# Gate and value products of an attention and GLU kernel's last batch by a seven-product scheme on 2x2 blocks

## The chip, the cores and the metric

The kernel runs on one core of one Trainium2 chip. The metric is the device time of a run in microseconds (us), median over runs; a profile of one execution gives the span from its first to its last instruction, and what each engine did in it. The engines are TensorE (PE in the rows, its weight loads PEld), VectorE (DVE), ScalarE (ACT), GpSimd (POOL) and SyncE (SP), which issues the DMAs here.

## The reference, cut to what matters

Attention on pairwise averaged queries, then a gated product of its result with three weight matrices, all in float32.

```python
B, H, S, D = 4, 8, 1152, 64                    # q, k, v
q_pool = q.reshape(B, H, S // 2, 2, D).mean(axis=3)
attn = softmax(q_pool @ k.T / sqrt(D))         # 576 x 1152 for each head
x = (attn @ v).transpose(0, 2, 1, 3).reshape(2304, 512)
gate = 1.0 / (1.0 + np.exp(-(x @ w_gate)))     # w_gate, w_val: 512 x 1536
out = (gate * (x @ w_val)) @ w_out             # w_out: 1536 x 512
```

## The kernel before

A float32 operand is held as two float32r parts, high and low, and a product is three matmuls into one PSUM bank: high x high, high x low, low x high. Attention goes by pairs of heads (16 pairs `p`, four to a batch) and by halves of 288 queries (`GR`, `GN = 288`). `normalise` writes each pair's result to a tile `x` with its two parts: 128 features, 576 tokens. Four such tiles are the 512 features of one batch.

`gated(ch, ...)` does the products of batch `ch`. Three times (`for th in range(3)`) it takes four of the twelve rows of 128 hidden features: for each row gate and value (`s`), two halves of tokens (`hf`) and four blocks of features (`kc`), three matmuls each; then the output product of these four rows, for four blocks `dm` of the result and two halves. A value product is multiplied with the gate on VectorE (line 895), copied to its high part on ScalarE (line 899), and POOL takes the low part (line 903) into a tile `g`, of which there are four. The output products are summed on VectorE (line 931) and stored after the last third. Weights come in by SyncE from a DRAM copy `w_d` that holds both parts: gate and value weights into three tiles `wg`, output weights into two tiles `wo`, in the last batch into the three pairs `K` (KA, KB) that attention has left by then:

```python
            tag = "K" if kind == "wo" and ch == B - 1 else kind
            wh = pl.hold(tag)
```

Nothing is ordered by hand. Each piece of work is declared with an engine, a guessed duration, a due time and what it must follow (`pl.op`), and each buffer as a slot of a tag (`SLOTS`, `pl.hold`). `Plan.run` lists all of it in time by these guesses, `Plan.search` shuffles due times and keeps what ends earlier, and the resulting order is the program order of every engine; an engine keeps to it. So products of one batch stand among the attention of the next, and what the last batch needs stands alone at the end. There are eight PSUM banks `b`.

Line 646 is the part of attention in which VectorE forms the low part of the exponentials (`el`), lines 465 and 481 form low parts of queries and keys, line 675 on POOL adds up rows of exponentials, and line 804 is a ScalarE copy of 512 weight columns.

## Time and profile before

| | |
|---|---|
| median of 3 runs | 920.87 us (919.88 to 922.19) |
| the profiled execution, first to last instruction | 919.1 us, 1.77 under the median; no other time of this execution is given |
| instructions | 18605 |
| busy: TensorE, VectorE, ScalarE, POOL | 910.0, 649.5, 657.5, 671.1 us |
| TensorE's granted clock | 1.00 of full speed throughout |

Busy times of matmuls overlap each other, since they are pipelined: what a matmul takes is read from how many start in a stretch. In a row of a group stand the line, the engine, the operation, what is written and read, the shape, the count, then the busy time in us and the mean duration in ns, then the idle time of the engine before these instructions and what ended it.

### The profile page before, as it was taken

The page shows a single profiled execution, that of the slowest core. Times are in us where ns is not written, and L with a number is a line of the kernel's source. Part 1 is how long each engine was busy: PE and PEld are TensorE (multiplying, and loading weights), DVE is VectorE, ACT ScalarE, POOL GpSimd, SP SyncE. Part 2 cuts the span into 40 slices and gives each one's busy share as a digit, 9 for nine tenths or more (in the row PEclk, how much of TensorE's full clock was granted, in tenths as well). Part 3 has the DMA queues.
Part 4 walks back from the last instruction along what each step waited for, and adds up shares of the span by engine and source line. Part 5 has one row for each costly group of instructions (what it writes and reads, how often), then busy time and mean ns, then how long its engine had stood idle before and what let it go on. Part 6 is the DMA issues. An engine that isn't in the chain of part 4 may idle for free.

```text
span 919.1 us, 18605 instructions
## 1 busy us (share of the span) xinstructions
PE 910.0 (99%) x6371; PEld 882.8 (96%) x6371; DVE 649.5 (71%) x1427; ACT 657.5 (72%) x1703; POOL 671.1 (73%) x669
## 2 busy tenths in 40 slices
PE   8999999999999999999999999999999999999998
PEld 8888888999999999999999999999999999999998
DVE  6677779888898987878787878877777874510112
ACT  4798899989998886777887677677877767422111
POOL 6765366889888989889899888888889877521211
PEclk9999999999999999999999999999999999999999
DMA  6899888788868666555644455554545423435432
GB/s 140 212 289 247 275 254 261 239 266 273 262 210 275 206 202 192 161 157 149 166 136 142 131 157 157 160 148 132 166 123 158 142 93 115 166 139 183 162 115 75
DMA packets 57616, 166.27 MB, mean 181 GB/s; under 512 B 17393, under 2 KB 21745, under 8 KB 51377
## 3 DMA queue, kind: packets, MB, share of 16 engines
q1 hardware_dynamic: 57360, 164.78, 59.3%
q8 instruction: 50, 0.82, 0.4%
q10 hardware_dynamic: 160, 0.30, 0.1%
q14 instruction: 46, 0.37, 0.1%
HBM read 132.12 MB, written 23.59 MB: 169 GB/s over the span
## 4 chain that ended last, share of the span: by engine, by line
PE 91%; ACT 4%; DVE 3%; POOL 1%; DMA 1%; issue 1%; POOLq 0%; ACTq 0%; DVEq 0%
PE bank L846 47%; PE bank L610 15%; PE bank L504 7%; PE bank L628 7%; PE bank L657 6%; PE bank L653 6%; PE bank L730 1%; DVE pm L417 1%; PE bank L951 1%; DMA wg<-wg_d 1%; ACT eh L614 1%; ACT bank L643 0%; ACT KA L475 0%; DMA wo<-wo_d 0%; DVE el L646 0%
## 5 line engine op out<-in xcount | busy, mean ns | idle before, releaser
L846 PE MATMUL bank<-x,wg 128*128 128x288 f32 x2304 | 353.8, 295 | 0.0
L846 PEld LDWEIGHTS bank<-x,wg 128*128 128x128 f32 x2304 | 325.6, 188 | 1.1 <-ACT sg L889 0.4
L646 DVE TENSOR_TENSOR el<-bank,eh 128x288 fp32r<-128x288 f32 x432 | 192.9, 452 | 70.7 <-ACT bank L643 65.9
L510 DVE TENSOR_REDUCE pm<-bank 128x1 f32<-128x384 f32 (+1 forms) x375 | 199.7, 550 | 49.6 <-PE bank L504 45.0
L614 ACT ACTIVATE eh<-bank 128x288 fp32r<-128x288 f32 x432 | 176.4, 409 | 73.1 <-PE bank L610 65.9
L643 ACT ACTIVATE bank<-bank 128x288 f32<-128x288 f32 x432 | 176.9, 410 | 0.2
L610 PE MATMUL bank<-QA,KA 128*128 128x288 f32 x576 | 175.1, 308 | 1.5 <-DVE pm L510 0.9
L610 PE MATMUL bank<-QB,KB 128*128 128x288 f32 x576 | 167.4, 295 | 0.0
L903 POOL TENSOR_TENSOR g<-sg,g 128x288 fp32r<-128x288 f32 x96 | 79.9, 833 | 105.2 <-ACT g L899 102.7
L675 POOL TENSOR_TENSOR acc<-acc,eh 128x576 f32<-128x576 f32 x92 | 132.5, 1440 | 16.7 <-ACT eh L614 14.6
L846 PE MATMUL bank<-g,wo 128*128 128x288 f32 x864 | 139.2, 295 | 0.2
L657 PE MATMUL bank<-el,vt 128*128 128x288 f32 x432 | 127.2, 296 | 0.5 <-DVE el L646 0.5
L653 PE MATMUL bank<-eh,vt 128*128 128x288 f32 x432 | 127.3, 296 | 0.0
L846 PEld LDWEIGHTS bank<-g,wo 128*128 128x128 f32 x864 | 125.0, 188 | 1.2 <-DMA wo<-wo_d 0.3
L504 PE MATMUL bank<-KA,QA 128*128 128x384 f32 (+1 forms) x375 | 125.7, 350 | 0.2
L610 PEld LDWEIGHTS bank<-QA,KA 128*128 128x128 f32 x576 | 108.2, 188 | 5.9 <-DVE pm L510 1.3
L610 PEld LDWEIGHTS bank<-QB,KB 128*128 128x128 f32 x576 | 108.3, 188 | 1.3
L895 DVE SCALAR_TENSOR_TENSOR sg<-sg,bank 128x288 f32<-128x288 f32 x96 | 43.3, 451 | 81.2 <-PE bank L846 79.2
L657 PEld LDWEIGHTS bank<-el,vt 128*128 128x128 f32 x432 | 81.1, 188 | 1.5 <-DVE el L646 1.2
L653 PEld LDWEIGHTS bank<-eh,vt 128*128 128x128 f32 x432 | 81.1, 188 | 0.7 <-ACT eh L614 0.3
L675 POOL TENSOR_TENSOR acc<-eh,eh 128x576 f32<-128x576 f32 x48 | 68.7, 1431 | 15.6 <-ACT eh L614 10.9
L628 PE MATMUL bank<-e,ve 128*128 128x288 f32 x288 | 76.6, 407 | 0.0
(86 smaller groups left out, 1359.6 us busy)
## 6 DMA issues: line engine op xcount, KB each, us to landing
wg<-wg_d SPq DMA_DIRECT2D x48, 1024.0 KB, 5.2
wo<-wo_d SPq DMA_DIRECT2D x36, 512.0 KB, 3.9
kr<-in_kT_dram SPq DMA_DIRECT2D x62, 288.0 KB, 5.0
wg_d<-cs SPq DMA_DIRECT2D x24, 512.0 KB, 5.0
qr<-in_qT_dram SPq DMA_DIRECT2D x31, 288.0 KB, 4.1
KP<-KA SPq DMA_DIRECT2D x30, 288.0 KB, 4.4
vr<-in_v_dram SPq DMA_DIRECT2D x24, 288.0 KB, 3.1
cr<-in_wg_dram SPq DMA_DIRECT2D x12, 512.0 KB, 5.3
```

What stands on the lines that cost most here:

```text
L504: nc.tensor.matmul(out=tl(m)[LO if t == 4 else ALL, 0:384], lhsT=lhs(t), rhs=rhs()[:, j * 384:(j + 1) * 384], start=True, stop=True)
L510: nc.vector.tensor_reduce(out=o, in_=tl(m)[p, 0:384], axis=AXX, op=ALU.max)
L610: nc.tensor.matmul(out=tl(m)[:, 0:GN], lhsT=tl(hd["k"])[k][:, ks], rhs=tl(hd["q"])[k][:, a:b], start=(k == 0), stop=(k == 1))
L614: nc.scalar.activation(out=ev(), in_=tl(m)[:, 0:GN], func=ACTF.Exp, scale=1.0 / 16.0)
L628: nc.tensor.matmul(out=tl(av[0])[:, 0:GN], lhsT=pair(c, 0), rhs=tl(h), start=(c == 0), stop=(c == NC - 1))
L643: nc.scalar.activation(out=p, in_=p, func=ACTF.Exp, scale=1.0 / 16.0)
L646: nc.vector.tensor_tensor(out=tl(el), in0=tl(m)[:, 0:GN], in1=ev().bitcast(F32), op=ALU.subtract)
L653: nc.tensor.matmul(out=tl(av[0])[:, 0:GN], lhsT=pair(c, w), rhs=ev(), start=(c == 0), stop=(c == NC - 1))
L657: nc.tensor.matmul(out=tl(av[1])[:, 0:GN], lhsT=pair(c, 1 - w), rhs=tl(el), start=(c == 0), stop=(c == NC - 1 and not mine_c))
L675: nc.gpsimd.tensor_tensor(out=tl(acc), in0=tl(old).bitcast(F32), in1=tl(eh).bitcast(F32), op=ALU.add)
L846: nc.tensor.matmul(out=ps[:, 0:GN], lhsT=l, rhs=r, start=(n == 0 and j == 0), stop=(n == 3 and j == 2))
L903: nc.gpsimd.tensor_tensor(out=g[:, 1, a:b], in0=tl(sg), in1=g[:, 0, a:b].bitcast(F32), op=ALU.subtract)
```

## The change

Batches 0 to 2 are as before. In the last batch two rows of hidden features and the 512 features of `x` make a 2x2 block matrix of weights (A11 to A22, blocks of 128 hidden by 256 features), and the features and the two token halves make a 2x2 matrix of `x` (B11 to B22). Seven block products take the place of eight: A11·B11, A12·B21, A22·T4, S1·T1, S2·T2, S3·T3, S4·B22, each of two K halves of 128 features and three matmuls.

The token blocks T1 to T4 are formed once, in `differences`, for the last two pairs: VectorE subtracts in float32, ScalarE makes the high and VectorE the low part. They lie in tiles that attention has left (Q, KP; the float32 work in vr). The weight blocks S1 to S4 are formed twelve times, in `combinations`: VectorE adds high and low part of two rows (line 950) and forms four sums of 256 columns in tile `kr` (line 953); ScalarE copies the high parts and POOL subtracts for the low parts (line 970), into one of the three pairs K. The plain weight rows come into `wg` as before, every fourth into `vt0` and `vt1`. The results are put together on VectorE: from one bank and a running sum in `sg` (line 1014), or within the bank (line 1050), before tanh (gate) or line 1073 (value, as line 895 before). Output weights of the last batch now use the two tiles `wo`.

```diff
+    def differences(p, j, me, nm, s):
+        if j == 0:
+            tb.update({"1": pl.hold("Q"), "2": pl.hold("Q"), "3": pl.hold("KP"), "4": pl.hold("Q"), "f": pl.hold("vr")})
+        old, fh = xs[p - 2, 0], tb["f"]
+        t1 = lambda: tl(fh).rearrange("p c d -> p (c d)")[:, GN * j:GN * j + GN]
+        b1 = lambda l, g: tl(old)[:, l, GN * g:GN * g + GN].bitcast(F32)
+        b21, b22 = (lambda: tl(me)[:, 0:GN]), (lambda: tl(me)[:, GN:SQ])
...
+        o = mix(t1, lambda: b1(0, 1), lambda: b1(0, 0), ALU.subtract, [old] + ([fh] if j else []),
+                [x_done[p - 2, 0], x_done[p - 2, 1]], s - 2, [] if j else [fh])
+        o = mix(t1, t1, lambda: b1(1, 1), ALU.add, [old, fh], [o], s - 2)
+        o = mix(t1, t1, lambda: b1(1, 0), ALU.subtract, [old, fh], [o], s - 2)
+        s1 = split("1", t1, [fh], [o], s)
+        t2 = mix(t1, b22, t1, ALU.subtract, [me, fh], [nm, s1], s)
+        split("2", t1, [fh], [t2], s + 0.1)
+        o = mix(b22, b22, lambda: b1(0, 1), ALU.subtract, [me, old], [t2, x_done[p, 1]], s + 0.1)
+        t3 = mix(b22, b22, lambda: b1(1, 1), ALU.subtract, [me, old], [o], s + 0.1)
+        t4 = mix(b21, b21, t1, ALU.subtract, [me, fh], [t2, x_done[p, 0]], s + 0.2)
+        split("3", b22, [me], [t3], s + 0.2)
+        split("4", b21, [me], [t4], s + 0.3)
...
-            tag = "K" if kind == "wo" and ch == B - 1 else kind
-            wh = pl.hold(tag)
+            wh = pl.hold(kind)
...
+            whs = [pl.hold("vt0"), pl.hold("vt1")] if m_ % 4 == 3 else [pl.hold("wg")]
...
+            fh, sh = pl.hold("kr"), pl.hold("K")
...
+            def full(w, h):
+                nc.vector.tensor_tensor(out=f(h, A), in0=w(0, s, A).bitcast(F32), in1=w(1, s, A).bitcast(F32), op=ALU.add)
+
+            def mix(out, in0, in1, op, after):
+                return pl.op("DVE", dve(256), lambda: nc.vector.tensor_tensor(out=f(*out), in0=f(*in0), in1=f(*in1), op=op),
...
+            r0 = pl.op("DVE", dve(512), lambda: full(a0, f0), at - 7, after=[l0], uses=w0, take=[fh])
+            r1 = pl.op("DVE", dve(512), lambda: full(a1, f1), at - 7, after=[l1], uses=w1 + [fh])
+            s1 = mix((f1, R), (f1, L), (f1, R), ALU.add, [r1])
+            s3 = mix((f1, L), (f0, L), (f1, L), ALU.subtract, [r0, s1])
+            s2 = mix((f0, L), (f1, R), (f0, L), ALU.subtract, [s1, s3])
+            s4 = mix((f0, R), (f0, R), (f0, L), ALU.subtract, [s2])
...
+                o = pl.op("ACT", act(512), hi, at - 6, after=after, uses=[fh] + ([sh] if k else []), take=[] if k else [sh])
+                done.append(pl.op("POOL", pool(512), lo, at - 6, after=[o], uses=[fh, sh]))
...
+            return {"A11": (w0, plain_w(a0, 0), l0), "A12": (w0, plain_w(a0, 256), l0), "A22": (w1, plain_w(a1, 256), l1),
+                    "S3": ([sh], mixed(0, 0), done[0]), "S1": ([sh], mixed(0, 256), done[0]),
+                    "S2": ([sh], mixed(1, 0), done[1]), "S4": ([sh], mixed(1, 256), done[1])}
...
+                    def mm(j=j, x=x):
+                        for c, (h, l) in enumerate(((0, 0), (0, 1), (1, 0))):
+                            nc.tensor.matmul(out=tl(bank)[:, 0:GN], lhsT=w(h, j), rhs=x(l),
+                                             start=(j == 0 and c == 0), stop=(j == 1 and c == 2))
+
+                    last = pl.op("PE", 3 * pe(GN), mm, at + 0.05 * j, after=[last, lw, xd],
+                                 uses=wh + [xh] + ([bank] if j else []), take=[] if j else [bank])
+                return bank, last, at
...
+            b, p, at = mult("A11", "11")
+            k1 = keep(s1, b, [p], at)
+            b, p, at = mult("S2", "T2")
+            k2 = plus(s2, b, s1, [p, k1], at)
+            b, p, at = mult("A12", "21")
+            put(0, 0, b, s1, [p, k1], at)
+            b, p, at = mult("S1", "T1")
+            k4 = plus(s4, b, s2, [p, k2], at)
+            b, p, at = mult("S3", "T3")
+            u2 = plus(s2, b, s2, [p, k2, k4], at)
+            put(1, 1, b, s4, [p, k4, u2], at)
+            b, p, at = mult("S4", "22")
+            put(0, 1, b, s4, [p, k4], at)
+            b, p, at = mult("A22", "T4")
+            put(1, 0, b, s2, [p, u2], at)
...
+                o = add(bank, sh, after, at)
+                done[r, hf] = pl.op("ACT", act(GN), tanh, at - 1, after=[o], uses=[bank] + ([] if new else [f]), take=[f] if new else [])
...
+        for third in range(3):
             gs = {}
-            for m_ in range(4 * th, 4 * th + 4):
+            if ch == B - 1:
+                two_rows(2 * third, gs)
+                two_rows(2 * third + 1, gs)
+            for m_ in range(4 * third, 4 * third + 4 if ch < B - 1 else 0):
```

The matmul's program line was 846 and is 892 for what stays and 1004 for the seven products. On TensorE, the first third was, before, one product after the other with the plain weights (`wg1`, then `wg2`) and the four `x` tiles:

```order
L846 MATMUL bank_69<-x7_128,wg1_133 128x288 x3
L846 MATMUL bank_69<-x0_3945,wg1_133 128x288 x3
L846 MATMUL bank_69<-x1_3946,wg1_133 128x288 x3
L846 MATMUL bank_69<-x6_127,wg2_134 128x288 x3
L846 MATMUL bank_69<-x7_128,wg2_134 128x288 x3
```

Now, the value products of the first two rows, from S1·T1 on (S1 and S3 in KA0, S2 and S4 in KB0, T1 to T4 in QA2 and QB2, QA0 and QB0, KP, QA1 and QB1):

```order
L1004 MATMUL bank_69<-QA2_82,KA0_74 128x288 x3
L1004 MATMUL bank_69<-QB2_85,KA0_74 128x288 x3
L1004 MATMUL bank_69<-KP_116,KA0_74 128x288 x3
L1004 MATMUL bank_69<-QA0_80,KB0_77 128x288 x3
L1004 MATMUL bank_69<-QB0_83,KB0_77 128x288 x3
L1004 MATMUL bank_69<-KP_116,KA0_74 128x288 x3
L1004 MATMUL bank_69<-x0_3921,KB0_77 128x288 x3
L1004 MATMUL bank_69<-x1_3922,KB0_77 128x288 x3
L1004 MATMUL bank_69<-QA1_81,wg1_133 128x288 x3
L1004 MATMUL bank_69<-QB1_84,wg1_133 128x288 x3
```

Eight of these ten rows read a weight sum or a token block that VectorE has made, and the rows are not in the order of the seven products but in the order in which the planner expects their operands.

On VectorE, the same stage was, before, from the end of the attention on (`opart` the last output products of batch 2, `sg` the value products of the last batch):

```order
L931 SCALAR_TENSOR_TENSOR opart2_131<-bank_69,opart2_131 128x288
L931 SCALAR_TENSOR_TENSOR opart3_132<-bank_69,opart3_132 128x288 x2
L895 SCALAR_TENSOR_TENSOR sg0_142<-sg0_142,bank_69 128x288
L895 SCALAR_TENSOR_TENSOR sg1_143<-sg1_143,bank_69 128x288
L895 SCALAR_TENSOR_TENSOR sg2_144<-sg2_144,bank_69 128x288
```

Now, from the sums for the second pair's gate on, with what each waits for:

```order
L950 TENSOR_TENSOR kr0_86<-wg2_134 128x512 [waits DMAHW7_49,Pool_49]
L950 TENSOR_TENSOR kr0_86<-vt00_89 128x512 [waits DMAHW4_49]
L1014 TENSOR_TENSOR sg2_144<-bank_69,sg0_142 128x288 [waits PE_49]
L953 TENSOR_TENSOR kr0_86<-kr0_86 128x256 [waits DVE_49] x4
L1014 TENSOR_TENSOR sg1_143<-bank_69,sg2_144 128x288
L1014 TENSOR_TENSOR sg2_144<-bank_69,sg2_144 128x288 [waits DVE_49,PE_49]
L1050 TENSOR_TENSOR bank_69<-bank_69,sg1_143 128x288
L1073 SCALAR_TENSOR_TENSOR t0_102<-t0_102,bank_69 128x288 [waits DVE_49,Activation_49]
L1050 TENSOR_TENSOR bank_69<-bank_69,sg1_143 128x288 [waits PE_49]
L1073 SCALAR_TENSOR_TENSOR acc0_99<-acc0_99,bank_69 128x288 [waits DVE_49,Activation_49]
L1050 TENSOR_TENSOR bank_69<-bank_69,sg2_144 128x288 [waits PE_49]
```

The first row waits for POOL to leave `kr`, and the additions that free banks stand behind it.

On SyncE, the last output weights were, before, loaded into three tiles in turn:

```order
L862 DMA KA0_74<-wo_d_146 128x1024
L862 DMA KA1_75<-wo_d_146 128x1024
L862 DMA KA2_76<-wo_d_146 128x1024
L862 DMA KA0_74<-wo_d_146 128x1024
L862 DMA wg2_134<-wg_d_145 128x2048
L942 DMA out_0_dram<-opart0_129 128x288
L862 DMA KA1_75<-wo_d_146 128x1024
```

Now they are loaded into two (these rows begin with the last third's first load):

```order
L906 DMA wo0_135<-wo_d_146 128x1024
L906 DMA wo1_136<-wo_d_146 128x1024
L906 DMA wo0_135<-wo_d_146 128x1024
L1170 DMA out_0_dram<-opart0_129 128x288 x2
L906 DMA wo1_136<-wo_d_146 128x1024
L1170 DMA out_0_dram<-opart1_130 128x288 x2
```

The third and the fourth load each go into a tile that the first and the second block of the same third have just read.

## Rows read from the trace of the kernel before

**Rows 1.** The page's part 1: busy us, share of the span, instructions.

```profile
span 919.1 us, 18605 instructions
...
PE 910.0 (99%) x6371; PEld 882.8 (96%) x6371; DVE 649.5 (71%) x1427; ACT 657.5 (72%) x1703; POOL 671.1 (73%) x669
```

**Rows 2.** Windows of the run: busy us and rows of each engine, granted clock.

```profile
core 0: us, PE busy (x) PEld busy (x) DVE busy (x) ACT busy (x) POOL busy (x), PEclk, DMA share, GB/s
...
500.00:600.00 100.00, 99.81 (x735) 99.30 (x734) 81.62 (x184) 73.08 (x196) 86.50 (x85) 1.00 0.55 162
...
740.00:760.00 20.00, 20.00 (x149) 20.00 (x148) 15.90 (x38) 14.79 (x40) 15.70 (x19) 1.00 0.24 93
760.00:780.00 20.00, 20.00 (x153) 20.00 (x153) 9.08 (x22) 14.38 (x42) 14.52 (x15) 1.00 0.36 132
...
820.00:840.00 20.00, 20.00 (x153) 20.00 (x152) 1.36 (x3) 5.04 (x12) 3.22 (x4) 1.00 0.52 185
```

**Rows 3.** The chain that ended last, from 850 us on.

```profile
849.89 66.01 PE bank L846 x498
...
915.93 0.46 DVE opart L931
```

**Rows 4.** Groups by line and shape, 787 us to the end.

```profile
L846 PE MATMUL bank<-x,wg 128*128 128x288 f32 x576 | 77.0, 295 | 0.0
...
L903 POOL TENSOR_TENSOR g<-sg,g 128x288 fp32r<-128x288 f32 x24 | 19.4, 807 | 84.6 <-ACT g L899 84.6
...
L931 DVE SCALAR_TENSOR_TENSOR opart<-bank,opart 128x288 f32<-128x288 f32 x24 | 11.0, 457 | 24.1 <-PE bank L846 24.0
L895 DVE SCALAR_TENSOR_TENSOR sg<-sg,bank 128x288 f32<-128x288 f32 x24 | 10.9, 454 | 76.7 <-PE bank L846 76.7
```

**Rows 5.** Groups by line and shape, the whole run.

```profile
L646 DVE TENSOR_TENSOR el<-bank,eh 128x288 fp32r<-128x288 f32 x432 | 192.9, 452 | 70.7 <-ACT bank L643 65.9 <-PE bank L504 0.3
...
L675 POOL TENSOR_TENSOR acc<-eh,eh 128x576 f32<-128x576 f32 x48 | 68.7, 1431 | 15.6 <-ACT eh L614 10.9 <-PE bank L504 2.1 <-PE bank L846 1.0
...
L804 ACT ACTIVATE cs<-bank 128x512 fp32r<-128x512 f32 x36 | 21.5, 609 | 0.3 <-DVE bank L800 0.2
...
L481 DVE TENSOR_TENSOR KB<-kr,KA 64x576 fp32r<-64x576 f32 x16 | 16.3, 1019 | 0.5
...
L465 DVE TENSOR_TENSOR QA<-qr,QA 64x576 fp32r<-64x576 f32 x16 | 15.3, 955 | 1.0 <-ACT opart L929 0.5
...
L370 DVE TENSOR_TENSOR qr<-qr 64x384 f32<-64x384 f32 x1 | 0.6, 550 | 1.9 <-DMA qr<-in_qT_dram 1.9
...
L370 DVE TENSOR_TENSOR qr<-qr 64x192 f32<-64x192 f32 x1 | 0.4, 351 | 0.4 <-DMA qr<-in_qT_dram 0.4
```

**Rows 6.** Line 481 on VectorE: duration in ns, min, median, max.

```profile
L481 DVE TENSOR_TENSOR KB<-kr,KA x16: 755/963/1925, 323.5 to 727.3; 64x576 fp32r<-64x576 f32 x16
```

**Rows 7.** VectorE in order of time: start us, duration us, and the instruction.

```profile
252.01 0.45 DVE L646 TENSOR_TENSOR el<-bank,eh 128x288 fp32r<-128x288 f32 x1
252.38 0.45 DVE L895 SCALAR_TENSOR_TENSOR sg<-sg,bank 128x288 f32<-128x288 f32 x1
...
253.90 0.46 DVE L646 TENSOR_TENSOR el<-bank,eh 128x288 fp32r<-128x288 f32 x1
254.39 0.46 DVE L709 TENSOR_TENSOR y<-bank,t 64x288 f32<-64x288 f32 x1
```

**Rows 8.** All engines in order of time, after one value product.

```profile
846.03 0.46 DVE L895 SCALAR_TENSOR_TENSOR sg<-sg,bank 128x288 f32<-128x288 f32 x1 [1.14 <-PE bank L846]
846.52 0.44 ACT L899 ACTIVATE g<-sg 128x288 fp32r<-128x288 f32 x1 [1.15 <-DVE sg L895]
847.11 0.81 POOL L903 TENSOR_TENSOR g<-sg,g 128x288 fp32r<-128x288 f32 x1 [0.78 <-ACT g L899]
```

**Rows 9.** DMA issues: count, KB each, median us from issue to landing.

```profile
wo<-wo_d SPq DMA_DIRECT2D x36, 512.0 KB, 3.9
...
KA<-wo_d SPq DMA_DIRECT2D x12, 512.0 KB, 3.3
```

More of the change, by code (lines that the diff above doesn't have):

```diff
@@ L757, in mult @@
             nc.gpsimd.tensor_tensor(out=y, in0=y, in1=tl(st["r"])[:, a:b], op=ALU.mult)
-        nm = pl.op("DVE", 1.2 if NMP(p) else 1.65, norm, s, after=st["yo"][g], uses=[st["y"], st["r"]], take=[th])
+        nm = pl.op("DVE", 1.2 if NMP(p) else 1.65, norm, s, after=st["yo"][g], uses=[st["y"], st["r"]], take=[tth])
         if NMP(p):
@@ L831, in gated, with now @@
         acc = {}
[L833 to L835 removed]
+        def now(n=1.0):
+            n_g[0] += n
+            return base + step * (n_g[0] - n)
         def product(at, parts, uses, after):
@@ new lines, in seven, with mult, plus, add @@
+        def seven(i, s, put):
+            sw = combinations(i, s)
+            s1, s2, s4 = (pl.hold("sg") for _ in range(3))
+            def mult(wname, name):
+                at = now(0.5)
+                wh, w, lw = sw[wname]
+                bank, last = pl.hold("b"), None
+                for j in range(2):
+                    if name in ("11", "21", "22"):
+                        p, hf = 4 * ch + 2 * (name[0] == "2") + j, int(name[1] == "2")
+                        xh, xd = xs[p, 0], x_done[p, hf]
+                        x = lambda l, xh=xh, hf=hf: tl(xh)[:, l, hf * GN:hf * GN + GN]
+                    else:
+                        xh, xd = tb[name[1]], x_done[name, j]
+                        x = lambda l, xh=xh, j=j: t_block(xh, j)[:, l]
+                    def mm(j=j, x=x):
[5 more added lines that the diff above has]
+                return bank, last, at
+            def plus(out, bank, sh, after, at):
+                def add():
+                    nc.vector.tensor_tensor(out=tl(out), in0=tl(bank)[:, 0:GN], in1=tl(sh), op=ALU.add)
+                return pl.op("DVE", dve(GN), add, at - 1, after=after, uses=[bank, sh],
+                             take=[] if out is sh else [out])
+            def keep(out, bank, after, at):
+                def copy():
+                    nc.scalar.activation(out=tl(out), in_=tl(bank)[:, 0:GN], func=ACTF.Copy)
+                return pl.op("ACT", act(GN), copy, at - 1, after=after, uses=[bank], take=[out])
+            b, p, at = mult("A11", "11")
[13 more added lines that the diff above has]
+            put(1, 0, b, s2, [p, u2], at)
@@ L911, in gated @@
             for dm in range(4):
-                wh, wt, lw = weights("wo", 4 * th + dm, base + step * n_g[0])
-                if th == 0:
+                wh, wt, lw = weights("wo", 4 * third + dm, base + step * n_g[0])
+                if third == 0:
                     acc[dm] = [pl.hold("opart"), [None, None]]
@@ L938, in gated @@
                     prev[hf] = o
-                    if th == 2:
+                    if third == 2:
                         def store(dm=dm, oh=oh, a=a, b=b):
@@ L978, in attention_glu_kernel @@
             pl.op("SP", 0.0, change_pools, PB + 1, after=[o for l in stored.values() for o in l], uses=blocked)
+        for some in later:
+            differences(*some)
         gated(b, PB * (b + 1), PB)
```

113 lines of the change are left out of this document (101 added, 12 removed).

## The prediction

> **What bounds the kernel now.** First the page's busy line: TensorE is busy 910.0 of 919.1 us, the next engines about 73% [rows 1]. A sum over stages hides where there is room, so the windows come second: from 740 us on TensorE is busy 20.00 of 20 at granted clock 1.00 (the 2.4 GHz level), while VectorE falls from 15.90 (740 to 760) to 1.36 (820 to 840), when the last batch's products are all that is left [rows 2]. Third, the chain that ended last: 66.01 us of nothing but 498 matmuls of line 846, then one VectorE instruction of 0.46 us and its store [rows 3]. So in the last stage a matmul less is time less, and a product of 128x288 costs 66.01 / 498 = 0.1326 us (the 295 ns in the groups overlap each other). The other engines wait there: lines 895 and 931 for TensorE nearly all the time [rows 4].
>
> **The part removed.** Before, the last batch's gate and value products are the 576 matmuls of [rows 4]. After, six pairs of weight rows x gate or value x seven products x two halves of K x three float32r terms = 504. 72 x 0.1326 = **9.55 us**, and TensorE has no idle time there that could swallow it.
>
> **What VectorE gets.** One third of the stage is four weight rows and their share of the output product: 168 + 96 = 264 matmuls, 35.0 us. VectorE does in it, before: eight of line 895 and eight of line 931, 8 x 0.454 + 8 x 0.457 = 7.3 us [rows 4]. After, for each of four combinations (line 950 twice on 512 columns, line 953 four times on 256): no row has these shapes, but line 370 takes 351 and 550 ns for 192 and 384 columns [rows 5], 1.04 ns a column, and the shortest 576 of line 481, 755 ns [rows 6], lies on that line; so 0.68 and 0.42, together 3.04 us. For each of the 28 products one addition out of a bank at line 646's 0.452 [rows 5]. Sum: 4 x 3.04 + 28 x 0.452 + 7.3 = **32.1 us against TensorE's 35.0**. Independent instructions start 0.37 apart, dependent ones 0.49 [rows 7], so full durations are a fair middle. VectorE goes from 7.3 of 38.2 us (288 matmuls), 19%, to 92% of the stage and stays 2.9 us a third under TensorE: hidden on the average, with little left. POOL: eight of 512 columns, between 0.807 at 288 and 1.431 at 576 [rows 4, 5], so 1.29, and eight of 0.807: 16.8 of 35.0. ScalarE gets four copies of at most 0.61 [rows 5] a pair of weight rows and is not near a bound.
>
> **How a sum comes in time.** One combination is 2 x 0.68 + 2 x 0.42 on VectorE, a ScalarE copy of at most 0.61, two POOL subtractions of 1.29 that follow each other, and handovers of 0.03 and 0.15 between engines [rows 8]: about 5.6 us from first addition to last low part, and tile kr is held throughout. TensorE eats one in 42 matmuls, 5.6 us. They tie, and three K pairs let the sums run ahead only while output products (12.7 us a third) run. Following the change's order with these durations from the attention's end, I find S products late by about 0.4 us in the first third, when the second pair's sums follow the first's additions, and not after. The first addition of the next sum waits for POOL to free kr, and behind it on VectorE stand additions that free banks; that is the place where 0.4 could grow (the second rival).
>
> **Collisions.** All sums of weights have both inputs in SBUF, as lines 481 and 465 on VectorE. These average 1.019 and 0.955 against a shortest of 0.755, with one of 1.925 [rows 5, 6]: 0.20 to 0.26 us extra, in stretches where POOL is busy 86.5% [rows 2]. The stage's POOL share is 16.8 / 35.0 = 48%, so some 0.13 each: 24 x 0.13 = 3.1 us a third, just the slack. I charge TensorE 0.5 a third, **1.5 us**; bounds 0, and 24 x 0.26 less 2.9 = 3.3 a third, 10.
> The Trainium skill, SBUF — State Buffer, "Who interferes with whom", says that a VectorE instruction with two SBUF inputs and a GpSimd instruction that reads SBUF exclude each other for the whole instruction; the spread of line 481 agrees in kind. By that rule, if every one of the 72 waited for half a POOL subtraction at a 48% chance, it would be 0.31 us each, 22 us: a slower kernel, about 925 us.
>
> **Token sums.** 14 differences and 8 low parts for each of the last two pairs' blocks, 22 x 0.45 = 9.9 us, and the first weight sum of 3.0, lie before the attention's end, where VectorE has 4.1 + 10.9 us free in 740 to 780 [rows 2]. Cost 0; uncovered, each would hold an `el` and so TensorE by 0.45. Behind the last normalisation the first T2 product waits for a difference, a copy and a low part (0.45 + 0.44 + 0.45) where x waited for copy and POOL (0.44 + 0.81) [rows 4, 8], one handover more, with 36 matmuls of cover in the order: 0.2, bounds 0 and 1.
>
> **The end of the last third.** After the last S2·T2 come 27 matmuls; VectorE has eleven instructions for them, 5.0 us, then the copy and the low part, 1.4 with handovers: 6.4 us before the last g is there. TensorE has 27 + 18 matmuls, 6.0: **0.5 us** of wait, in a place that had none. And the output weights: before, three KA tiles; now two wo tiles, and dm 2 can be loaded only when dm 0's last matmul is over. 24 matmuls, 3.2 us, must hide a transfer of 3.3 (KA) to 3.9 us (wo) [rows 9]: **0.4**, bounds 0.1 and 0.9. In the first two thirds other products stand between.
>
> **The rest of the program** is put in a new order by the same planner, since all queues are planned at once. TensorE is idle there about 0.2% (99.81 of 100 in 500 to 600 [rows 2]); I take 0, and 1 us to both sides.
>
> **Sum.** -9.55 + 0.4 + 1.5 + 0.2 + 0.5 + 0.4 = -6.55: span 919.1 to 912.55. The median of the runs, 920.87, is 1.77 above this span; the profiled execution has no other time of its own. **914.3 us.**
>
> **Rivals.**
> *All of it arrives.* No wait but the 0.5 at the end: -9.0, 911.8. For it: VectorE's sum is still under TensorE's. Against: two chains tie with TensorE.
> *Each sum is late.* The tie breaks the wrong way: each of twelve combinations is late by 0.5 us (one VectorE addition ahead of it in the queue), 6 us instead of 1.9: 918.4, no difference to speak of. For it: kr is single and VectorE keeps its order. Against: output products give every third 12.7 us to catch up.
> *VectorE becomes the bound.* It decides where the 72 weight sums wait for POOL by more than (3 x 2.9 + 9.55) / 72 = 0.25 us each; at 0.35, between line 481's mean and its longest, the stage is 25.2 - 18.2 = 7 us longer than before: 928, slower. For it: rows 6 and 92% before any wait. Against: POOL is half as busy as where these rows come from.
> The rule in the section on collisions is this rival.
>
> **Numbers.** Chances: forecast 0.65 (its bounds: 910.8 with every wait at its lower end and 1 us of luck in the new order, 917.5 with collisions at 4.5), all 0.15, late sums 0.13, VectorE 0.07. A measurement of this kernel tells about 0.3% from no change, 2.8 us: faster is under 918.1. The first two and a quarter of the third are faster, 0.82; the third's remainder and little else the same, 0.10; slower 0.08. Range 910.8 to 919.5, leaving out the top of the late sums and the slow case.
>
> **What would show it.** In the changed profile: 504 matmuls of the new line; TensorE nearly unbroken from 790 us on with VectorE at 85 to 95%; lines 950 and 953 at 0.68 and 0.42 with a tail; waits of TensorE for POOL on KA and KB under 2 us in all; a wait for wo near the end. Wrong would be TensorE waiting for VectorE's additions (banks) all through the stage, or lines 950 and 953 at half again their price, or losses of more than 1 us before 740.

## The result, and the profile after

The change made the kernel slower: 930.51 us, median of four runs (929.62 to 931.79), against 921.25 us for the kernel before on the same chip, a ratio of 1.0101 (95% interval 1.0087 to 1.0115): 1% slower. The forecast was 914.3. The profiled execution spans 929.6 us, 10.5 more than the one before. The 72 matmuls are gone (6371 before, now 6299), and with them 9.55 us; so 20.0 us were lost somewhere in this execution (18.8 by the medians).

The busy line of the page after, the answer to [rows 1]:

```profile
PE 909.1 (98%) x6299; PEld 873.3 (94%) x6299; DVE 742.1 (80%) x1605; ACT 679.3 (73%) x1747; POOL 706.7 (76%) x693
```

TensorE has 72 matmuls less and is busy just as long: the busy time of matmuls that overlap doesn't tell what was saved. The windows do, by their counts. The stretches of [rows 2] in the kernel after (columns: window; length; busy us and count of TensorE, its weight loads, VectorE, ScalarE, POOL; granted clock; DMA share and GB/s):

```profile
740.00:760.00 20.00, 19.11 (x136) 18.43 (x135) 16.92 (x39) 11.66 (x33) 13.88 (x16) 1.00 0.14 40
760.00:780.00 20.00, 18.24 (x132) 17.38 (x131) 17.70 (x35) 14.02 (x41) 15.89 (x16) 1.00 0.25 98
820.00:840.00 20.00, 19.23 (x136) 18.04 (x136) 19.07 (x43) 8.74 (x20) 11.79 (x10) 1.00 0.62 219
```

A full stretch of 20 us held 153 matmuls before. Now it is 136, 132 and 136, with the clock at 1.00 throughout, and VectorE is busy 16.92 to 19.07 of 20. Three wider windows give the account, first of before, then of after:

```profile
740.00:820.00 80.00, 79.91 (x597) 79.47 (x596) 40.09 (x93) 43.62 (x119) 46.97 (x51) 1.00 0.37 131
820.00:900.00 80.00, 80.00 (x606) 80.00 (x605) 11.38 (x25) 17.85 (x42) 14.52 (x18) 1.00 0.41 145
900.00:930.00 30.00, 15.89 (x120) 15.66 (x119) 4.57 (x10) 1.30 (x3) 1.61 (x2) 0.99 0.18 57
```

```profile
740.00:820.00 80.00, 75.68 (x548) 73.41 (x547) 65.04 (x135) 47.34 (x131) 54.60 (x54) 1.00 0.34 114
820.00:900.00 80.00, 76.99 (x566) 75.28 (x566) 69.79 (x148) 32.42 (x72) 43.26 (x37) 1.00 0.45 160
900.00:930.00 30.00, 24.19 (x175) 23.11 (x173) 14.18 (x35) 5.65 (x14) 6.45 (x8) 0.98 0.26 75
```

From 740 us to the end the old kernel has 597 + 606 + 120 = 1323 matmuls in these windows. The new one, if it were as far at 740, would have 72 fewer, 1251; it has 1289. (A matmul under way at an edge counts in both windows, which cancels where kernels are compared; a single entry is good to some 0.3 us.) It is 38 matmuls behind there, 38 x 0.1326 = 5.0 us, in a part of the program that the change doesn't touch. Behind 740, a stretch's loss is its length less 0.1326 for each matmul in it (for the last, the span's end less 900): 7.3, 4.9 and 6.4 us, against 0.8, -0.4 and 3.2 before. So: **before 740 5.0, attention's end (740 to 820) 6.5, the stage (820 to 900) 5.3, the end 3.2: 20.0 us.** The forecast had 0, 0.2, 1.9 and 0.9. The same account for every run below, less the row of before:

| run | median us, ratio to before (95%) | behind at 740 | 740 to 820 | 820 to 900 | from 900 |
|---|---|---|---|---|---|
| the change | 930.51, 1.0101 (1.0087 to 1.0115) | 5.0 | 6.5 | 5.3 | 3.2 |
| e1, old kernel, other draw | 925.83, 1.0057 (1.0042 to 1.0072) | 5.0 | -0.7 | 0.0 | -0.1 |
| e2, change, other draw | 927.99, 1.0078 (1.0063 to 1.0094) | -1.2 | 11.0 | 1.1 | 3.4 |
| e3, change, old order to 690 | 923.29, 1.0028 (1.0016 to 1.0040) | 0.9 | 5.3 | 2.3 | 3.5 |
| e4, change's order, tokens one input | 927.20, 1.0073 (1.0058 to 1.0088) | 4.4 | 1.7 | 6.4 | 2.9 |
| e5, e3's order, POOL reads less | 921.20, 1.0006 (0.9997 to 1.0016) | 1.1 | 5.0 | 0.4 | 3.2 |
| e6, e5 and tokens one input | 918.18, 0.9975 (0.9965 to 0.9985) | 2.7 | 1.9 | 1.1 | 3.1 |
| e7, e3 and wo early, new order | 929.84, 1.0096 (1.0079 to 1.0113) | 1.3 | 11.8 | 2.1 | 3.9 |
| e8, e3 and weight sums in banks | 919.99, 0.9992 (0.9982 to 1.0001) | -0.1 | 2.9 | 2.7 | 3.2 |
| e9, e8 and token sums in banks | 925.05, 1.0052 (1.0040 to 1.0065) | 1.2 | 4.9 | 2.5 | 4.8 |
| e10, e9 and wo early | 920.64, 1.0007 (0.9998 to 1.0016) | 0.7 | 3.5 | 2.7 | 2.0 |
| e11, e3 with dearer sums | 933.16, 1.0139 (1.0126 to 1.0153) | 0.8 | 6.2 | 4.8 | 10.2 |
| e12, e3's order and wo early | 922.19, 1.0020 (1.0011 to 1.0029) | 0.9 | 5.2 | 2.4 | 1.9 |
| e13, e8 and wo early, longer search | 920.89, 1.0000 (0.9991 to 1.0009) | 1.7 | 6.2 | 0.7 | 1.1 |
| e14, e13 and token sums in banks | 916.73, 0.9956 (0.9944 to 0.9968) | 1.1 | 1.3 | 3.1 | 1.5 |
| e15, e13's order, tokens one input | 915.17, 0.9940 (0.9926 to 0.9953) | 0.5 | 1.5 | 1.9 | -0.1 |

The columns are of one execution each: those of the change, e6 and e14 lie 1.3, 1.9 and 1.5 us above their medians and that of e2 2.2 below, so these rows are that much high or low. The windows are fixed in time, not in the program: a kernel that is earlier has a piece of the end already in the column of the stage (e8 and e14 below).

Where the three later losses come from is seen in the trace after. VectorE's groups from 690 us on (columns: line, operation, what is written and read, shapes, count; busy us, mean ns; idle before and who ended it):

```profile
L953 DVE TENSOR_TENSOR kr<-kr 128x256 f32<-128x256 f32 x48 | 27.6, 575 | 1.1
L1050 DVE TENSOR_TENSOR bank<-bank,sg 128x288 f32<-128x288 f32 x48 | 20.7, 457 | 0.0
L950 DVE TENSOR_TENSOR kr<-wg 128x512 f32<-128x512 f32 x18 | 15.1, 851 | 6.2 <-POOL KB L970 6.2
L807 DVE TENSOR_TENSOR vr<-vr,x 128x288 f32<-128x288 f32 x4 | 3.5, 862 | 0.1
L807 DVE TENSOR_TENSOR y<-y,x 128x288 f32<-128x288 f32 x4 | 2.6, 646 | 0.1
L800 DVE TENSOR_TENSOR QA<-vr,QA 128x288 fp32r<-128x288 f32 x2 | 2.0, 980 | 0.9 <-ACT QA L796 0.9
L807 DVE TENSOR_TENSOR y<-y,vr 128x288 f32<-128x288 f32 x2 | 1.9, 946 | 0.1
...
L800 DVE TENSOR_TENSOR KP<-y,KP 128x288 fp32r<-128x288 f32 x2 | 0.9, 450 | 0.1
```

Line 1050, with one input from a bank, takes 457 ns at 288 columns. The 22 token sums of the same width with both inputs in SBUF (lines 807 and 800) take anything from 448 to 980 by group, 15.7 us in all, 0.71 each, where 22 x 0.45 would be 9.9; and line 953, which the forecast priced at 0.42 us bare, 575. One of them in time, with VectorE and POOL (columns: start, us, engine, line, operation):

```profile
752.20 1.43 POOL L675 TENSOR_TENSOR acc<-eh,eh 128x576 f32<-128x576 f32 x1 [1.34 <-ACT eh L614]
752.34 1.61 DVE L807 TENSOR_TENSOR vr<-vr,x 128x288 f32<-128x288 f32 x1
753.97 0.46 DVE L646 TENSOR_TENSOR el<-bank,eh 128x288 fp32r<-128x288 f32 x1
```

The token sum starts 0.14 us after POOL's sum of exponentials and ends 0.32 after it: it gets hardly anything done until POOL is through. Behind it stands an `el` of attention, and TensorE's next row is this:

```profile
754.49 0.45 PE L504 MATMUL bank<-KA,QA 128*128 128x384 f32 x1 [0.87 <-DVE el L646]
```

By the Trainium skill, SBUF — State Buffer, "Who interferes with whom", a VectorE instruction with two inputs in SBUF contends with a GpSimd instruction that reads SBUF, over a port pair that is an exclusive lock. The trace agrees: 1.61 us where 0.46 is the bare time, with 1.29 us of POOL's 1.43 inside it.

TensorE's waits from 740 us on (columns: who waited for whom; us in all, times, longest):

```profile
PE bank L892 <- ACT acc L1063: 1.9, 1, 1.9
PE bank L892 <- DMA wo<-wo_d: 1.9, 3, 0.9
PE bank L657 <- DVE el L646: 1.3, 3, 0.6
PE bank L892 <- DVE pm L510: 1.0, 1, 1.0
PE bank L504 <- DVE el L646: 0.9, 1, 0.9
```

The first is at 846.91. The chain of work that ended last leads to it (columns: start, us, what):

```profile
842.61 0.93 DVE kr L953
...
843.56 0.93 DVE kr L953
...
844.51 1.39 DVE kr L953
...
845.92 0.39 ACT KB L966
...
846.46 0.40 ACT acc L1063
...
846.91 3.19 PE bank L892 x22
```

Three weight sums of 0.42 took 3.25 us beside POOL's low parts of `g` and of `KA`; the ScalarE copy of their result (line 966) stands in ScalarE's queue ahead of a tanh that frees a bank (line 1063), and TensorE wants that bank.

### The profile page after: what moved, and what is told of

Read it like the earlier page. It is cut to its first block, busy times and chain, and to the rows that moved or that the text cites. A ratio compares the mean times of both kernels' runs of the same rounds, so it can differ in the third digit from the quotient of the medians.

```text
span 929.6 us, 18751 instructions
## 1 busy us (share of the span) xinstructions
PE 909.1 (98%) x6299; PEld 873.3 (94%) x6299; DVE 742.1 (80%) x1605; ACT 679.3 (73%) x1747; POOL 706.7 (76%) x693
## 4 chain that ended last, share of the span: by engine, by line
PE 78%; DVE 9%; ACT 5%; POOL 4%; DMA 2%; issue 2%; SPq 0%; DVEq 0%; POOLq 0%; ACTq 0%
PE bank L892 35%; PE bank L610 14%; PE bank L504 7%; PE bank L628 7%; PE bank L657 5%; PE bank L653 5%; PE bank L1004 3%; DMA kr<-in_kT_dram 2%; PE bank L730 1%; DVE kr L953 1%; ACT eh L614 1%; DVE kr L950 1%; DVE pm L417 1%; ACT KA L475 1%; DVE sg L1014 1%
## 5 line engine op out<-in xcount | busy, mean ns | idle before, releaser
L892 PE MATMUL bank<-x,wg 128*128 128x288 f32 x1728 | 277.1, 295 | 1.0 <-DVE pm L510 1.0
L892 PEld LDWEIGHTS bank<-x,wg 128*128 128x128 f32 x1728 | 248.8, 188 | 2.4 <-DVE pm L510 1.3
L892 PE MATMUL bank<-g,wo 128*128 128x288 f32 x1152 | 178.3, 295 | 4.7 <-ACT acc L1063 1.9
L610 PE MATMUL bank<-QA,KA 128*128 128x288 f32 x576 | 177.2, 312 | 2.0 <-DVE el L646 1.0
L892 PEld LDWEIGHTS bank<-g,wo 128*128 128x128 f32 x1152 | 162.8, 188 | 6.5 <-ACT acc L1063 2.1
L1131 POOL TENSOR_TENSOR g<-sg,g 128x288 fp32r<-128x288 f32 x72 | 59.6, 827 | 23.0 <-ACT g L1127 21.9
L504 PEld LDWEIGHTS bank<-KA,QA 128*128 128x128 f32 (+1 forms) x375 | 69.0, 187 | 5.8 <-DVE el L646 1.7
```

The costliest lines, as they stand in the source:

```text
L504: nc.tensor.matmul(out=tl(m)[LO if t == 4 else ALL, 0:384], lhsT=lhs(t), rhs=rhs()[:, j * 384:(j + 1) * 384], start=True, stop=True)
L610: nc.tensor.matmul(out=tl(m)[:, 0:GN], lhsT=tl(hd["k"])[k][:, ks], rhs=tl(hd["q"])[k][:, a:b], start=(k == 0), stop=(k == 1))
L892: nc.tensor.matmul(out=ps[:, 0:GN], lhsT=l, rhs=r, start=(n == 0 and j == 0), stop=(n == 3 and j == 2))
L1131: nc.gpsimd.tensor_tensor(out=g[:, 1, a:b], in0=tl(sg), in1=g[:, 0, a:b].bitcast(F32), op=ALU.subtract)
```

## The experiments

All were timed in alternation with the kernel before (920.5 to 920.8 us, 920.57 in e1 to e4).

### Is it the order? e1 to e3

The planner draws random numbers to vary its due times. In e1 and e2 only the draw differs, in the old kernel and in the changed one; e3 gives the changed kernel the due times that the old one ended with, for the 6713 pieces of work that both have in common, and lets the search touch only what comes behind 690 us.

```diff
-        dice = random.Random(1)
+        dice = random.Random(2)          # e1 (old kernel), e2 (changed kernel)
```

```diff
+        for o, due in zip(self.ops, DUE):   # e3: due times of the old kernel
+            o.prio = due
         best = self.run()
...
-            at = dice.uniform(-width, end)
+            at = dice.uniform(690.0, end)
```

> The kernel before, its planner's shuffles drawn from another seed: same instructions, another order on every engine. If the 5 us that the changed kernel has lost by 740 us (38 matmuls behind) are the luck of a new order, a new order of the old kernel moves its time by some us as well, either way: 917 to 927 us. If order matters little and the loss comes from the change itself, 920 to 922 us.

> The changed kernel with the same other seed. Luck of the order: 924 to 936 us, and a different number of matmuls behind at 740 us. Loss by the change itself: 929.5 to 931.5 us, again some 38 matmuls behind at 740 us.

> The changed kernel, with all work up to the last batch's products put in the order of the kernel before (its due times taken over) and the shuffles allowed only from 690 us on. If the order cost the 5 us before 740 us: those come back, 925 to 926 us, the last stage as long as in the changed kernel. If the change itself holds up the work before 740 us: 929 to 931 us.

e1: 925.83, 5.3 us slower than the same kernel with the first draw, nearly all of it before 740. e2: 927.99, even at 740, but 11.0 lost at attention's end. e3: 923.29, below both of its theories; 7.2 us come back, 4.1 of them before 740 and 3.0 in the stage, which was expected to stay as long as it was. So 4 to 5 us of the change's loss are an order that came out worse in a part that the change doesn't touch, and the old kernel can lose them as well. In the stage, too, the order counts for some 3. It also means that two versions whose orders differ are not comparable to better than some 5 us; where it can be done, the runs below keep an order.

### Do sums with two inputs in SBUF collide with POOL? e4 to e6

e4 keeps the change's order, and the 22 VectorE instructions of the token blocks read one input: copies stand for the differences, which are left out. e5 keeps e3's order, and POOL's low part of the mixed weights is two memsets, which read nothing; these low parts are left out. e6 is e5 with e4's edit. Both edits take away more than the input: what is not read is not waited for. In e5 `kr` no longer waits for POOL to have read it, and the low parts need no mixed sum; in e4 and e6 a low part need not wait for ScalarE's copy (1.1 us of VectorE's time in the change, none in e5).

```diff
-nc.vector.tensor_tensor(out=out(), in0=in0(), in1=in1(), op=op)
+nc.vector.tensor_reduce(out=out(), in_=in0().unsqueeze(2), axis=AXX, op=ALU.max)      # e4, e6
...
-nc.gpsimd.tensor_tensor(out=t[:, 512:1024], in0=f(h, A), in1=t[:, 0:512].bitcast(F32), op=ALU.subtract)
+for _ in range(2):                                                                    # e5, e6
+    nc.gpsimd.memset(t[:, 512:1024].bitcast(F32), 0.0)
```

> The changed kernel in its own order, but the 22 VectorE instructions for the token blocks read one operand from SBUF and copy it (the differences are left out). If two operands in SBUF collide with POOL and this is what holds up the attention's end (6.9 us lost from 740 to 820 us): these instructions take 0.45 us each, 4 to 6 us come back, 925 to 926.5 us. If their mere number in VectorE's queue does it: no more than 1.5 us back, 929 to 931 us.

> e3_same_head with one thing changed, in the same order of instructions: GpSimd's subtraction that forms the rounded-off low part of the mixed weights (L970 of the changed kernel, 24 times, 1.28 us each) is replaced by two memsets of the same tile, which read nothing; the low parts of the mixed weights are left out. If VectorE's sums with two inputs in SBUF are held up by GpSimd's reads (theory: collisions), most weight sums return to their bare 0.37 and 0.64 us, except beside GpSimd's other reads, and of the 4.2 us that TensorE loses in e3 from 800 to 900 us, 2 to 3 come back: 920.3 to 921.3. If what holds TensorE up there is that the sums fill VectorE however long they take (rival), less than 1 us comes back: 922.4 to 923.3.

> As e5_head_nopool, and besides the 22 VectorE instructions that form the token blocks read one input instead of two (as in e4_tokens_one_input; differences left out), in the order of e3_same_head. Theory: attention's end gives back 2.5 to 4 us more, so 917 to 918.5, and what is left above 911.8 is the end of the last third (about 3 us) and the rest of attention's end. Rival (it is the count of instructions on VectorE, not their length): within 1 us of e5_head_nopool.

e4: 927.20, 3.3 us less, between its two theories; 740 to 820 goes from 6.5 to 1.7, while the stage loses 1.1 more (in this execution the granted clock is 0.71 from 840 to 844 us). The groups of e4, from 690 us on, against 980 and 862 above:

```profile
L800 DVE TENSOR_REDUCE QA<-vr 128x288 fp32r<-128x288 f32 x2 | 0.9, 444 | 0.4 <-PE bank L610 0.4
L807 DVE TENSOR_REDUCE vr<-vr 128x288 f32<-128x288 f32 x4 | 1.8, 445 | 0.1
```

As many instructions of the same width, and half the time: it is not their number. e5: 921.20, 2.1 less than e3, and the stage's loss goes from 2.3 to 0.4. That is the time that its theory named, but hardly for its reason. Line 1119 (950 of the change), first in e3, then in e5:

```profile
L1119 DVE TENSOR_TENSOR kr<-wg 128x512 f32<-128x512 f32 x18 | 15.3, 862 | 7.2 <-POOL KB L1139 7.1
```

```profile
L1119 DVE TENSOR_TENSOR kr<-wg 128x512 f32<-128x512 f32 x18 | 15.4, 871 | 0.3 <-ACT KB L1135 0.3
```

These sums are no shorter than before; all 72 weight sums together take 42.9 us of VectorE instead of 44.9, since POOL still reads SBUF for the low parts of `g`. What is gone is the wait in front of them, 7.1 us for POOL to leave `kr`, and in e3 TensorE's waits for POOL's low parts in KA and KB, 0.60 and 0.87 us, which are most of the 1.9. So e5 measures above all POOL's place in the making of a sum, and of the collisions not more than a share that it doesn't tell apart. A collision can be seen in its trace, though, beside a sum that meets none (line 1250 is 1080 of the change):

```profile
820.94 0.90 DVE L1119 TENSOR_TENSOR kr<-wg 128x512 f32<-128x512 f32 x1
821.25 1.25 POOL L1250 TENSOR_TENSOR g<-acc,g 128x288 fp32r<-128x288 f32 x1
821.76 1.29 DVE L1119 TENSOR_TENSOR kr<-vt 128x512 f32<-128x512 f32 x1
822.46 1.25 POOL L1250 TENSOR_TENSOR g<-t,g 128x288 fp32r<-128x288 f32 x1
...
841.40 1.11 POOL L1140 MEMSET KB<- 128x512 f32 x2
...
841.99 0.68 DVE L1119 TENSOR_TENSOR kr<-wg 128x512 f32<-128x512 f32 x1
```

Beside a POOL instruction that reads SBUF a weight sum takes 1.29 us, beside memsets 0.68; and POOL's own instructions, 0.81 when alone, take 1.25 here. In the first four rows each instruction behind the first starts while the one above it runs, and is the longer for it: whoever is second waits. e6: 918.18, another 3.0 less, from attention's end (5.0 to 1.9): the 22 instructions take 9.9 us of VectorE instead of 13.7, and TensorE's wait of 1.1 us there for an `el` is gone. In one order, then, the token sums' second input costs 3.0 us, and POOL's low parts of the weight sums 2.1; without the two the change is ahead of the old kernel (0.9975).

### The end's wait for output weights: e7 and e12

The output weights of the third and fourth `dm` go into two of attention's four `eh` tiles, so that they are there in time. e7 lets the planner search a new order; e12 keeps e3's due times, which gives e3's order up to attention's end and nearly e3's behind.

```diff
+            if kind == "wo" and ch == B - 1 and m_ % 4 > 1:
+                whs = [pl.hold("eh"), pl.hold("eh")]
...
+                        nc.sync.dma_start(out=tl(whs[h]).rearrange("p l t -> p (l t)")[:, 0:512].bitcast(F32),
+                                          in_=w_d[kind][m_][:, h, 0])
```

> e3_same_head, and the output weights of the third and fourth 128 rows of each third of the last batch go into two of attention's free eh tiles instead of waiting for one of the two wo tiles. Theory: the two waits of TensorE for wo (0.92 and 0.28 us, and about 0.3 us of refilling behind each) go: 1.2 to 1.8 us less than e3's 923.3, so 921.5 to 922.1. Rival: SP's queue is late with those loads anyway, or the plan that comes out is another one: no gain within 0.5 us.

> e3_same_head with the output weights in attention's free tiles, as e7_head_wo_early, but with the due times that e3 ended with and no further search, so that the order is e3's up to attention's end and nearly e3's behind it. Theory (e7's loss is its order): the waits for output weights go, 921.3 to 922.3 against e3's 923.3. Rival (the loads or the tiles cost something themselves): 925 or more.

e7 missed both of its theories: 929.84, 6.5 us slower than e3, though TensorE no longer waits for wo. The loss stands at attention's end (11.8). e12 has the same loads into the same tiles and takes 922.19, 1.1 less than e3, with the end's loss down from 3.5 to 1.9: no wait for wo is left in its trace. (The intervals of the two overlap, 1.0011 to 1.0029 and 1.0016 to 1.0040; that e12 is not slower is sure, the 1.1 is not.) So e7's loss is its order. What that order did, in e7's trace (VectorE and POOL, then TensorE):

```profile
755.86 3.22 POOL L844 TENSOR_TENSOR acc<-acc,eh 128x576 f32<-128x576 f32 x2
...
757.74 2.61 DVE L976 TENSOR_TENSOR y<-y,x 128x288 f32<-128x288 f32 x2
759.15 0.89 POOL L851 TENSOR_TENSOR acc<-acc 128x288 f32<-128x288 f32 x1
760.28 0.45 DVE L815 TENSOR_TENSOR el<-bank,eh 128x288 fp32r<-128x288 f32 x1
...
760.78 0.40 PE L779 MATMUL bank<-QA,KA 128*128 128x288 f32 x1 [2.61 <-DVE el L815]
```

Two token sums beside POOL's additions take 2.61 us, an `el` stands behind them, and TensorE waits 2.61 us for that. The order is expensive by what happens to stand beside POOL.

### Can the planner be told? e11

```diff
-pl.op("DVE", dve(256), lambda: nc.vector.tensor_tensor(...
+pl.op("DVE", dve(256) + 0.2, lambda: nc.vector.tensor_tensor(...     # likewise lines 950, 800, 807
```

> e3_same_head, with the planner told 0.2 us more for each of VectorE's 94 sums with two inputs in SBUF, which is about what they took longer in the trace; nothing else changed. Theory (the order is built on prices that are too low): a better order, 1 to 3 us less than e3's 923.3. Rival: no price can say when GpSimd reads, and the order is luck: within 2 us either side, 921.5 to 925.5.

933.16, the slowest of all, outside both expectations. A higher average price drew yet another order, which loses 10.2 us from 900 on. Its trace shows TensorE there waiting 1.2 us for ScalarE's copy of a mixed weight, 1.1 for POOL's low part of it and 2.3 for ScalarE's copy of `g`, with the granted clock at 0.59 from 904 to 908 and 0.70 from 916 to 920. Why this order came out so is not shown. A likely reason that a price doesn't help, argued and not tested, is that a mean does not tell a planner beside what a sum will stand.

### Sums without a second input in SBUF: e8 to e10, e13 to e15

Here the sums themselves are changed. In e8 ScalarE copies the high parts of both weight rows into two PSUM banks (24 copies of 512 columns more), VectorE adds the low parts in the banks, and every later sum has one input in a bank. S2 is then A22 - S3 instead of S1 - A11, since two banks can't be the inputs of one instruction.

```diff
+    nc.scalar.activation(out=tl(bf[n]), in_=w(0, s, A).bitcast(F32), func=ACTF.Copy)
...
-    nc.vector.tensor_tensor(out=f(h, A), in0=w(0, s, A).bitcast(F32), in1=w(1, s, A).bitcast(F32), op=ALU.add)
+    nc.vector.tensor_tensor(out=out(), in0=b(n, cols), in1=w(1, s, cols).bitcast(F32), op=ALU.add)
...
+    s1 = mix((f1, R), lambda: f(f1, L), lambda: b(1, R), ALU.add, [r1, r2], 1)
+    s3 = mix((f1, L), lambda: b(0, L), lambda: f(f1, L), ALU.subtract, [r0, s1], 0)
+    s2 = mix((f0, L), lambda: b(1, R), lambda: f(f1, L), ALU.subtract, [s3], 1)
+    s4 = mix((f0, R), lambda: b(0, R), lambda: f(f0, L), ALU.subtract, [s2], 0)
```

e9, e10 and e14 form the token blocks in two banks for each pair too, beginning with a ScalarE copy (in e9 and e10 the fourth block is B21 - T1, which is wrong, whatever their expectations say of the whole result; in e14 it is B21 - T2 as in the change; the instructions are as many). e10, e13 and e14 also have e7's early output weights. e13 and e14 come from a longer search of the planner over the last 230 us. e15 is e13 in e13's order with e4's edit (differences left out).

```diff
+        o = pl.op("ACT", act(GN), lambda: nc.scalar.activation(out=t1(), in_=b1(0, 1), func=ACTF.Copy), s - 1,
+                  after=[x_done[p - 2, 0], x_done[p - 2, 1], nm], uses=[old], take=[b_1, b_2])
+        o = mix(t1, t1, lambda: b1(0, 0), ALU.subtract, [old, b_1], [o], s - 1)
...
+        t2 = mix(t2v, b22, t1, ALU.subtract, [me, b_1, b_2], [nm, o], s)
+        t4 = mix(t1, b21, t2v, ALU.subtract, [me, b_1, b_2], [s1, t2], s + 0.1)
+        o = mix(t2v, t2v, lambda: b1(0, 0), ALU.subtract, [b_2, old], [t4, s2], s + 0.1)
```

> e3_same_head, and the weight sums work on PSUM banks: ScalarE copies the high part of both weight tiles to two banks (24 copies of 512 more), and each of VectorE's sums has one input there and one in SBUF. The whole result is computed. Theory (collisions): every weight sum takes its bare 0.37 to 0.67 us whatever GpSimd does; as e5_head_nopool or up to 1 us less, 919.5 to 921.3. Rival: two of the eight banks held for about 4 us of every 14.8 make TensorE wait for banks, 924 or more.

> e8_head_sums_in_banks, and the token blocks too are formed in PSUM banks (two copies on ScalarE, then each of VectorE's 22 sums has one input in a bank and one in SBUF). The whole result is computed. Theory (collisions at attention's end): the 3 us that e6 gained over e5 come here too: 916.5 to 918.5 against e8's 920.0, below the kernel before (920.65). Rival: banks held in attention's end, where its own products want all eight, cost as much as the collisions did: 920 to 923.

> e9_head_all_sums_in_banks and the output weights in attention's free tiles as in e7_head_wo_early. Theory: with no sum left that GpSimd can hold up, the order matters little, so e7's loss does not come back and only its gain is left, 1.2 to 1.8 us against e9: 915 to 917. Rival: e7's loss came from the loads or the tiles themselves: again 5 us or more above e9.

> The weight sums of e8_head_sums_in_banks and the output weights of e7_head_wo_early, in an order from a longer search over the last 230 us. The whole result is computed. Theory: e8's 920.0 less the waits for output weights at the end, 917.5 to 919.3, faster than the kernel before by 0.15 to 0.35%. Rival: the order is luck by 2 us or more either way, 917 to 923, since the token sums still collide.

> As e13, and the token sums in banks too (as in e9 and e10, whose kernels computed the fourth token block from the wrong one of the two differences), in an order from a longer search of its own. The whole result is computed. Theory: no collision is left in the change, 915.5 to 918. Rival: the banks that the token blocks hold at attention's end cost what the collisions did, as in e9: 920 or more.

> e13_sums_in_banks_wo_early in its own order, with one input for each of the 22 VectorE instructions of the token blocks (differences left out, as in e4 and e6). Theory: 2.5 to 3.5 us less than e13, about 915; then what is left above 911.8 is about 3 us of order and of the last third's end. Rival: the token sums' collisions cost little in this order, within 1 us of e13.

e8: 919.99, 3.3 less than e3, as expected. Its weight sums, beside a POOL that reads as much as in the change (lines 1129 and 1133 are 950 and 953):

```profile
L1133 DVE TENSOR_TENSOR kr<-bank,kr 128x256 f32<-128x256 f32 x36 | 15.2, 422 | 1.5
L1129 DVE TENSOR_TENSOR bank<-bank,wg 128x512 f32<-128x512 f32 x12 | 8.3, 692 | 0.0
```

422 and 692 ns, against 575 and 851: the bare prices, with no collision left. The column of the stage says 2.7, more than in e3, but 1.6 of that are the waits for the last g, 1.1 and 0.5, which in this kernel come before 900 us and in e3 behind 903; without them it is 1.1 against 2.3. The rest of the gain stands at attention's end and before 740, so the order plays in, and no run here prices the weight sums' collisions alone. e9 came out at 925.05, beyond even its rival, and e10 at 920.64, above its theory of 915 to 917 but 4.4 below e9. e13 is no faster than the old kernel (1.0000, 0.9991 to 1.0009), which was its rival: it loses 6.2 us at attention's end, where the token sums still have two inputs and take 17.2 us. e15, the same order without them, takes 915.17: 5.7 us less, where 2.5 to 3.5 were expected, and attention's end goes from 6.2 to 1.5. And e14, which computes the whole result with every sum in banks, takes **916.73 us, 0.9956 of the kernel before (0.9944 to 0.9968)**: faster than both kernels. Its windows from 740 us on, and its token sums (line 1078 is 807):

```profile
740.00:820.00 80.00, 79.25 (x587) 78.29 (x586) 63.79 (x155) 55.30 (x147) 54.65 (x57) 1.00 0.46 154
820.00:900.00 80.00, 78.12 (x583) 77.27 (x582) 64.24 (x157) 40.47 (x90) 39.35 (x40) 1.00 0.38 132
```

```profile
L1078 DVE TENSOR_TENSOR bank<-bank,x 128x288 f32<-128x288 f32 x10 | 4.6, 462 | 0.2
L1071 DVE TENSOR_TENSOR QA<-bank,QA 128x288 fp32r<-128x288 f32 x3 | 1.4, 451 | 0.2 <-ACT QA L1067 0.2
```

VectorE has more instructions than in the change from 740 to 820 (155 against 135) and TensorE has 587 matmuls instead of 548. e9 and e14 differ in their order (and in what T4 is taken from), and are 8 us apart; whether banks held at a worse moment cost e9 its time was not tried apart.

## Why the prediction was wrong, point by point

**The part removed** held: 504 matmuls, 9.55 us; every run's account closes with it.

**"The rest of the program ... I take 0, and 1 us to both sides"** failed: 5.0 us before 740. The reason given, that TensorE is idle only 0.2% there, says what the old order does and nothing of a new one (losses of more than 1 us before 740 were named among the things that would make it wrong). e1 loses as much in the old kernel by another draw, e3 gets 4.1 back.

**"Token sums ... Cost 0"** failed, and it is the error of reading that matters most. 9.9 us of VectorE time were set against 4.1 + 10.9 us free, as if any moment would do. But these sums have two inputs in SBUF, in the stretch where POOL is busy 13.88 and 15.89 of 20 us and VectorE's `el` is what TensorE waits for next. The forecast had the price ("uncovered, each would hold an el and so TensorE by 0.45") and the collision's mean for instructions with two inputs in SBUF [rows 5, 6], but used the collision for the weight sums only. Measured: the 22 take 15.7 us, and 6.5 us are lost at attention's end, of which e4 gives back 4.8 there (3.3 of the median); e6 and e15 give back 3.2 and 4.8 of theirs.

**"Collisions" and "How a sum comes in time"**: 1.5 + 0.4 in all for the stage, 5.3 found in the change's order and 2.3 in e3's. The kind of delay was right, and the 0.13 us a weight sum nearly so: by the bare 422 and 692 ns of e8, line 953's 575 and line 950's 851 are 0.15 to 0.16 more each. Laying 3.1 us a third against 2.9 of slack was the step that failed: delays don't spread evenly, and three sums in a row at 842.61 took 2.0 us too long, with one wait of 1.9 behind them. The 0.4 for a sum that comes late was too small as well: the forecast named POOL holding `kr` as the place where it could grow, VectorE waits there for 6.2 us in the change, and e5, which takes this wait away and few of the collisions, gives back 1.9 in e3's order. How the two share the 5.3 stays open.

**"The end of the last third"**: 0.5 + 0.4 forecast, 3.2 found. The places were right. TensorE at the end of the kernel after, where [rows 3] had one unbroken piece:

```profile
911.65 0.40 PE L892 MATMUL bank<-g,wo 128*128 128x288 f32 x1 [0.41 <-ACT g L1077]
912.53 5.71 PE L892 MATMUL bank<-g,wo 128*128 128x288 f32 x41 [0.48 <-POOL g L1080]
919.16 3.42 PE L892 MATMUL bank<-g,wo 128*128 128x288 f32 x24 [0.93 <-DMA wo<-wo_d]
923.00 3.42 PE L892 MATMUL bank<-g,wo 128*128 128x288 f32 x24 [0.42 <-DMA wo<-wo_d]
```

The waits for g are 0.89 together, those for output weights 1.35, and behind each the pipeline refills (24 matmuls take 3.42 us instead of 3.18). e12 removes the output weights' part: 1.6 us of the account, 1.1 of the median, where 0.4 was forecast.

**The rivals.** "VectorE becomes the bound" (928) is nearest to the time, but not what happened: it needed 0.25 us for each of 72 sums, and they took 0.16. "Each sum is late" had the place that e5 shows to matter, but 4 us for it. The loss is spread over four places that no rival joined. The rule of the Trainium skill that the section on collisions named, SBUF — State Buffer, "Who interferes with whom", worked out there as 0.31 us a sum, was right in kind and too high for the weight sums; it should have been laid on the token sums first, which took 0.26 more each. Two small sums of the prediction are off (6.4 less 6.0 is 0.4, not 0.5; 914.3 with collisions at 4.5 is 917.3, not 917.5); nothing hangs on them.

**What stays open.** Which order the planner finds is luck of up to 8 us here (e9 and e14, e3 and e7). How collisions and POOL's hold on `kr` share the stage's loss was not taken apart. Of the 6.9 us that e14's execution still loses against a change that costs nothing, 1.1 lie before 740, 1.3 at attention's end, 1.5 in the two waits for the last g just before 900 us, and about as much behind them, where its granted clock is 0.57 (20 matmuls from 900 to 904, 32 in the next 4 us); the rest was not taken apart. The other four executions of e14 show 1.00 and take 915.84 to 916.95.

## What to carry to other kernels

Before you call work on VectorE hidden, look at where its inputs lie: a sum with both in SBUF, in a stretch where GpSimd reads SBUF, can take three times its price (1.61 us for 0.46 here), and what counts is who stands behind it in the queue. Putting one input into a PSUM bank gave the bare price back each time here, for a copy on an engine with room. When an experiment takes an input away, ask which wait goes with it: e5's time came as expected, and its trace gives another reason. And where a planner orders everything, hold the order fixed (or try another draw on the old kernel) before you believe a difference of less than a per cent.
